# A scheduler that starts its TensorE clock at one half, and five first memsets moved from VectorE to GpSimd

## The chip, the cores and the metric

The kernel runs on one core of a Trainium2 chip. Its time is the device time of one execution in microseconds (us). It was taken several times for each kernel; "span" is the time from the first to the last instruction in a profiled execution and is about 1.8 us shorter. The granted clock is the share of TensorE's full clock that the throttle granted, as the profile records it.

TensorE, written PE in the profile, multiplies matrices. VectorE is DVE, ScalarE is ACT, GpSimd is POOL, and SyncE (SP) issues transfers. PEld is TensorE's loading of weights.

## The reference

Two layers, each attention and then a gated feed-forward block, on 2048 rows of 512 numbers, 32 heads of 16:

```python
def _A_ref(x, wqkv, wo):                       # 32 heads, Dh = 16
    q, k, v = split(x @ wqkv)
    p = softmax(einsum("bhqd,bhkd->bhqk", q, k) * Dh ** -0.5)
    return merge(einsum("bhqk,bhkd->bhqd", p, v)) @ wo
def _B_ref(x, w_gate, w_up, w_down):           # F = 1792
    return (gelu(x @ w_gate) * (x @ w_up)) @ w_down
for _ in range(2):
    x = x + _A_ref(layernorm(x), A_wqkv, A_wo)
    x = x + _B_ref(layernorm(x), B_w_gate, B_w_up, B_w_down)
```

(`split` and `merge` stand for the reshapes and transposes, which are cut.)

## The kernel before

The kernel isn't written as a fixed order of instructions. A greedy list scheduler, in Python, models all engines and decides at each modelled moment what TensorE does next; the order that comes out is fixed when the program is built. A wrong cost in the model therefore makes no wrong result. It makes a different order.

Two parts matter here. The first is the model of TensorE's clock: in windows of 3.413 us it counts the work done, and the next window runs at full rate only if the last one was busy for at least 42.5%.

```python
HAM, LEAST, BACK = 3.413, 0.425, 0.425
ham = {"n": 0, "act": 0.0, "rate": 1.0}        # the first window's rate
...
def ham_to(n):
    while ham["n"] < n:
        share = ham["act"] / HAM
        ham["rate"] = 1.0 if share >= (LEAST if ham["rate"] == 1.0 else BACK) else 0.5
        ham["n"] += 1
        ham["act"] = 0.0
def pe_time(t, work):
    while True:
        ham_to(int((t + 1e-6) // HAM))
        end = (ham["n"] + 1) * HAM
        can = (end - t) * ham["rate"]
        if work <= can:
            ham["act"] += work
            return t + work / ham["rate"]
        ham["act"] += can
        work -= can
        t = end
```

The second is what TensorE does when nothing is ready. It multiplies zeros into the accumulator bank, to keep its clock up. One call makes a group of four matmuls, side by side on four column strips of the array, 512 columns each:

```python
def keep_clock():
    ones = AP(ONB, 0, [[128, 128], [0, 4], [1, 128]])
    def fn(e):
        for j in range(4):
            ins = e.matmul(PS[32 * j:32 * j + VW, ACC, :], lhsT=ZV[:, :], rhs=ones, start=False, stop=False,
                           tile_position=(0, 32 * j), skip_group_check=True)
        return ins
    pe(fn, [("ZV",), ("ONB",)], [BK[ACC]], MM, "col")      # MM = 0.216 us at full rate
...
# in the main loop, when no tile, no product and no piece of work is ready:
if acc["free"] and not over[0] and density(t) < DENSE and ...:     # DENSE = 0.7
    keep_clock()
```

The head of the kernel is a chain. Four row tiles of x (128 rows each) are loaded; VectorE takes their statistics; GpSimd makes the layernorm scales, two tiles at a time; VectorE applies them; TensorE transposes the rows; then come the first projections to K, Q and V, and the first products of Q and K. Only then can ScalarE start its first exp. The initial memsets stood on VectorE in front of those statistics:

```python
sch.op("dve", lambda e: e.memset(PS[:, ACC, :], 0.0), w=[BK[ACC]], cost=0.6)
sch.op("dve", lambda e: e.memset(AP(VP, 16, [[NKT * H * VW, 128], [VW, NKT * H]]), 1.0), w=[("VPONE",)], cost=0.6)
sch.op("dve", lambda e: e.memset(RB[:], 0.0), ...)
sch.op("dve", lambda e: e.memset(OKL[:], 1.0), ...)
sch.op("dve", lambda e: e.memset(OKV[:], 1.0), ...)
sch.op("dve", lambda e: e.memset(LT[:], 1.0), ...)
```

## Time and profile before

| | before |
|---|---|
| time, median | 1685.6 us (1682.91 to 1685.63, 3 runs) |
| span of the profiled run | 1682.9 us |
| ScalarE busy | 1561.6 us, 93% |
| first exp starts | 17.67 us |
| last exp ends | 1610.1 us |
| after it (output projection, last feed-forward) | 72.7 us |

The first view is the page. Its first part gives busy time, share of the span and instruction count per engine. The groups of its fifth part give line, engine, operation, output and inputs, shapes, count, busy time, mean ns of one, and idle time before them.

```profile
span 1682.9 us, 37093 instructions
...
PE 1576.2 (94%) x15611; PEld 492.6 (29%) x15670; DVE 1378.6 (82%) x2334; ACT 1561.6 (93%) x1348; POOL 203.4 (12%) x217
...
L1204 ACT ACTIVATE fPT<-fPS 128x1536 bf16<-128x1536 f32 (+1 forms) x1302 | 1487.9, 1284 | 46.3 <-PE fPS L1191 42.5
...
```

ScalarE does the exps for nearly the whole span (L1204), and TensorE feeds it. So what delays the first exp delays everything, unless some slack later takes it up.

The second view is the chain of waits of the kernel before over its first 20 us (start, length, what): the work that ended last, followed backwards.

```profile
1.52 10.41 PE fPS L1344 x141
11.93 0.55 PE fPS L569 x8
...
17.67 2.37 ACT fPT L1204 x2
```

Of the 17.67 us before the first exp, 10.41 are the dummy matmuls of L1344. The timeline of the same stretch (start, length, engine, line, operation, tiles, count, and in brackets the idle time before it and what ended that) shows what they covered:

```profile
1.52 10.41 PE L1344 MATMUL fPS<-fONB,fZV 128*17 128x512 f16 x144 [1.52 <-POOL fQMASK L362]
...
3.86 0.91 DVE L369 MEMSET fRB<- 128x1024 f32 x1
...
4.99 0.63 DVE L540 BATCH_NORM_STATS2 fST<-fX 128x6 f32<-128x512 bf16 x1
...
5.76 0.15 PEld L1344 LDWEIGHTS fPS<-fONB,fZV 128*17 128x17 f16 x4 [0.28 <-issue]
...
6.18 0.15 PEld L1344 LDWEIGHTS fPS<-fONB,fZV 128*17 128x17 f16 x4 [0.28 <-issue]
...
6.59 4.85 PEld L1344 LDWEIGHTS fPS<-fONB,fZV 128*17 128x17 f16 x92 [0.25 <-issue]
...
8.14 0.72 DVE L562 TENSOR_SCALAR fHT<-fX,fLNS 128x512 f16<-128x512 bf16 x2
...
9.78 0.74 DVE L562 TENSOR_SCALAR fHT<-fX,fLNS 128x512 f16<-128x512 bf16 x2 [0.92 <-POOL fLNS L552]
...
11.87 0.62 PE L569 MATMUL fPS<-fIDN,fHT 128*128 128x128 f16 x8
...
```

The reader should see three things. The weight loads of dummy groups come every 0.43 us (5.76, 6.18) until 6.6 us, after which 92 of them pass in 4.85 us, that is a group of four every 0.21 us: TensorE ran at half rate at first. The first two tiles' rows were normalised between 8.14 and 8.86 us. The transposes (L569) that need them started at 11.87, as the dummies ended.

### The profile page before, as it was taken

To read this page: it belongs to the slowest core of one execution; us is meant where nothing else is said; L and a number is where in the kernel's file an instruction comes from. 1 tells how busy PE (TensorE), PEld (TensorE's weight loads), DVE (VectorE), ACT (ScalarE), POOL (GpSimd) and SP (SyncE) were. 2 spreads that over 40 slices of the span, in tenths; PEclk is the share of its full clock that TensorE was granted. 3 is DMA by queue.
4 is the path that set the end of the run, shared out by engine and by line. 5 is a ranking of instruction groups with operands and counts; after the bars stand their busy time and mean duration, and the time that the engine had idled before them with its cause. 6 is when DMAs were issued, how large, how long until landed. Compare 5 with 4: busy or idle time off the path is not lost.

```text
span 1682.9 us, 37093 instructions
## 1 busy us (share of the span) xinstructions
PE 1576.2 (94%) x15611; PEld 492.6 (29%) x15670; DVE 1378.6 (82%) x2334; ACT 1561.6 (93%) x1348; POOL 203.4 (12%) x217
## 2 busy tenths in 40 slices
PE   9999989999999989999999999999989999999998
PEld 3332222222222223233332322222222222222233
DVE  7899998888998899977643899988899878897852
ACT  6899999999999999999899999999999999999922
POOL 2312011101201021000600211101011100201000
PEclk9999999999999999999999999999999999999999
DMA  4100001252013410125214000024301251014303
GB/s 138 52 2 19 2 19 33 61 164 73 17 43 119 144 42 10 41 66 170 74 57 138 26 19 17 21 58 136 108 19 39 68 166 57 17 45 146 109 15 109
DMA packets 140286, 111.82 MB, mean 66 GB/s; under 512 B 13905, under 2 KB 129873, under 8 KB 140113
## 3 DMA queue, kind: packets, MB, share of 16 engines
q1 hardware_dynamic: 136416, 104.78, 21.3%
q0 software_dynamic: 2112, 4.19, 0.9%
q8 instruction: 127, 2.08, 0.5%
q10 hardware_dynamic: 1584, 0.39, 0.1%
q14 instruction: 47, 0.38, 0.1%
HBM read 97.78 MB, written 6.82 MB: 62 GB/s over the span
## 4 chain that ended last, share of the span: by engine, by line
ACT 52%; PE 35%; DVE 10%; DMA 1%; issue 1%; SPq 1%; POOL 0%; POOLq 0%; DVEq 0%
ACT fPT L1204 49%; PE fPS L592 11%; PE fPS L1324 9%; PE fPS L1191 9%; DVE fPP L1277 4%; PE fPS L953 4%; DVE fPI L1241 3%; ACT fHT L1157 2%; PE fPS L1344 2%; DVE fHT L939 1%; SPq L277 1%; DVE fHT L916 1%; ACT L1157 1%; PE fPS L656 1%; DVE fQ L636 0%
## 5 line engine op out<-in xcount | busy, mean ns | idle before, releaser
L1204 ACT ACTIVATE fPT<-fPS 128x1536 bf16<-128x1536 f32 (+1 forms) x1302 | 1487.9, 1284 | 46.3 <-PE fPS L1191 42.5
L1241 DVE TENSOR_SCALAR fPI<-fPS 128x512 int16<-128x512 f32 x843 | 571.0, 684 | 93.4 <-PE fPS L1191 87.6
L1191 PE MATMUL fPS<-fQ,fKT 32*128 32x512 f16 x4096 | 513.2, 384 | 50.0 <-ACT fPT L1204 36.3
L1324 PE MATMUL fPS<-fPT,fVP 128*17 128x512 bf16 x3253 | 469.0, 382 | 11.7 <-DVE fOS L829 5.6
L1277 DVE TENSOR_SCALAR fPP<-fPI 128x2048 int16<-128x2048 int16 (+3 forms) x723 | 444.7, 645 | 8.1 <-PE fPS L1324 2.3
L1324 PE MATMUL fPS<-fPP,fVD 128*17 128x512 f16 x2529 | 409.7, 381 | 10.8 <-DVE fPP L1277 5.9
L1191 PEld LDWEIGHTS fPS<-fQ,fKT 32*128 32x128 f16 x4096 | 129.0, 91 | 533.7 <-ACT fPT L1204 382.4
L1324 PE MATMUL fPS<-fPI,fVP 128*17 128x512 f16 x843 | 255.0, 382 | 2.0 <-DVE fPP L1277 1.5
L592 PE MATMUL fPS<-fXNT,fWR 128*128 128x512 f16 x896 | 221.7, 381 | 10.4 <-DVE fHT L939 6.0
L1344 PE MATMUL fPS<-fONB,fZV 128*17 128x512 f16 x2452 | 189.6, 385 | 2.3 <-POOL fQMASK L362 1.5
L1324 PEld LDWEIGHTS fPS<-fPT,fVP 128*17 128x17 f16 x3253 | 108.7, 88 | 163.4 <-issue 91.6
L788 POOL TENSOR_TENSOR fAT<-fOS,fRB 128x512 f16<-128x512 f32 x32 | 41.3, 1291 | 817.2 <-DMA fRB<-rscr 791.6
L1324 PEld LDWEIGHTS fPS<-fPP,fVD 128*17 128x17 f16 x2529 | 99.3, 88 | 120.7 <-issue 48.5
L939 DVE TENSOR_TENSOR fHT<-fPS,fHT 128x512 bf16<-128x512 f32 x112 | 76.4, 689 | 57.8 <-PE fPS L592 41.4
L953 PE MATMUL fPS<-fWR,fHT 128*128 128x512 bf16 x402 | 113.5, 382 | 7.2 <-issue 5.7
L592 PEld LDWEIGHTS fPS<-fXNT,fWR 128*128 128x128 bf16 x896 | 72.8, 98 | 128.3 <-DVE fHT L939 19.6
L916 DVE CAST fHT<-fPS 128x512 bf16<-128x512 f32 x98 | 66.6, 687 | 25.6 <-PE fPS L592 25.2
L1344 PEld LDWEIGHTS fPS<-fONB,fZV 128*17 128x17 f16 x2452 | 57.8, 91 | 66.5 <-issue 31.2
L1324 PEld LDWEIGHTS fPS<-fPI,fVP 128*17 128x17 f16 x843 | 58.3, 88 | 38.0 <-issue 13.9
L669 POOL TENSOR_SCALAR fVD<-fVP 128x544 f16<-128x544 f16 (+1 forms) x48 | 54.7, 1142 | 97.0 <-DVE fVP L677 94.4
L548 POOL TENSOR_SCALAR fLNS<-fMV 128x4 f32<-128x4 f32 (+1 forms) x17 | 5.2, 307 | 434.8 <-DVE fMV L541 434.7
L788 POOL TENSOR_TENSOR fATS<-fOS,fRB 128x512 f16<-128x512 f32 x32 | 42.3, 1323 | 78.2 <-DMA fRB<-rscr 78.2
(60 smaller groups left out, 697.9 us busy)
## 6 DMA issues: line engine op xcount, KB each, us to landing
fWR<-in_B_w_down_dram SPq DMA_DIRECT2D x189, 256.0 KB, 3.0
fWR<-in_B_w_gate_dram SPq DMA_DIRECT2D x56, 256.0 KB, 3.3
fWR<-in_B_w_up_dram SPq DMA_DIRECT2D x56, 256.0 KB, 2.9
fRB<-rscr SPq DMA_DIRECT2D x256, 32.0 KB, 1.8
fX<-in_A_x_dram POOLq DMA_DIRECT2D x4, 1024.0 KB, 5.6
xscr<-fX SPq DMA_DIRECT2D x16, 256.0 KB, 2.5
fX<-xscr SPq DMA_DIRECT2D x4, 1024.0 KB, 5.7
fAT<-fATS SPq DMA_DIRECT2D x128, 16.0 KB, 1.8
```

Of the source, the lines that this page charges most:

```text
L592: ins = e.matmul(bank(bs[0])[:, 0:cols], lhsT=l, rhs=r_, start=(i == 0), stop=(i == n - 1))
L669: job("pool", 2, [(lambda e, dst=dst, src=src, ph=ph: e.tensor_scalar(dst, src, 2.0 ** (-ph / NPH), None, op0=ALU.mult), [("VP", c, k) for ...
L788: job("pool", 1, [(lambda e: e.tensor_tensor(dst, OS[:, os_, :], RB[:, slot, :], op=ALU.mult), [("OS", os_)] + [("RB", slot, j) for j in r ...
L916: evac_job(1, b, [(lambda e: e.tensor_copy(HT[:, ft, :], bank(b)), [BK[b]], [("HT", ft)], 0.6)], got(("gate", layer, qb, ft)))
L939: (lambda e: e.tensor_tensor(HT[:, ft, :], bank(b), HT[:, ft, :], op=ALU.mult), [BK[b], ("HT", ft)], [("HT", ft)], 0.62)], got(("up", laye ...
L953: ins = e.matmul(bank(b)[:, 0:D], lhsT=HT[:, ft, i * 128:(i + 1) * 128], rhs=WR[:, s, jj * D:(jj + 1) * D], start=(ft == 0), stop=(ft == N ...
L1191: ins = e.matmul(bank(b), lhsT=KT[32 * j:32 * j + 32, (u % NG) // 2, kt * 128:(kt + 1) * 128], rhs=Q[32 * j:32 * j + 32, (layer * NU + u) ...
L1204: o = sch.op("act", lambda e: e.activation(PT[:, p, 0:512 * na].rearrange("p (a b) -> p a b", a=na), PS[:, b0:b0 + na, :], ACTF.Exp, scale ...
L1241: dve(0, [(lambda e: e.tensor_scalar(PI[:, gi, 512 * r:512 * (r + 1)], bank(bd), DBIAS, 0.0, op0=ALU.add, op1=ALU.max), [BK[bd]], [("PI", ...
L1277: shifts.append((s, [(lambda e: e.tensor_scalar(PP[:, s, 0:512 * n], PI[:, gi, 0:512 * n], int(OCT) * ph // NPH, None, op0=ALU.add), [("PI ...
L1324: ins = e.matmul(PS[32 * j:32 * j + VW, ACC, :], lhsT=l, rhs=r_, start=a, stop=z, tile_position=(0, 32 * j), skip_group_check=True)
L1344: ins = e.matmul(PS[32 * j:32 * j + VW, ACC, :], lhsT=ZV[:, :], rhs=ones, start=False, stop=False, tile_position=(0, 32 * j), skip_group_c ...
```

## The change

Its intent is to make the model's clock true to the chip over the first microseconds, and to let VectorE reach its first statistics sooner. It is six lines:

```diff
-    ham = {"n": 0, "act": 0.0, "rate": 1.0}
+    ham = {"n": 0, "act": 0.0, "rate": 0.5}
...
     sch.op("dve", lambda e: e.memset(PS[:, ACC, :], 0.0), w=[BK[ACC]], cost=0.6)
-    sch.op("dve", lambda e: e.memset(AP(VP, 16, [[NKT * H * VW, 128], [VW, NKT * H]]), 1.0), w=[("VPONE",)], cost=0.6)
-    sch.op("dve", lambda e: e.memset(RB[:], 0.0), w=[("RB", i, j) for i in range(NRB) for j in range(4)], cost=0.6)
-    sch.op("dve", lambda e: e.memset(OKL[:], 1.0), w=[("OKL",)])
-    sch.op("dve", lambda e: e.memset(OKV[:], 1.0), w=[("OKV",)])
-    sch.op("dve", lambda e: e.memset(LT[:], 1.0), w=[("LT", i) for i in range(HB)])
+    sch.op("pool", lambda e: e.memset(OKV[:], 1.0), w=[("OKV",)])
+    sch.op("pool", lambda e: e.memset(AP(VP, 16, [[NKT * H * VW, 128], [VW, NKT * H]]), 1.0), w=[("VPONE",)], cost=0.9)
+    sch.op("pool", lambda e: e.memset(OKL[:], 1.0), w=[("OKL",)], cost=0.2)
+    sch.op("pool", lambda e: e.memset(LT[:], 1.0), w=[("LT", i) for i in range(HB)], cost=0.2)
+    sch.op("pool", lambda e: e.memset(RB[:], 0.0), w=[("RB", i, j) for i in range(NRB) for j in range(4)], cost=0.9)
```

## The prediction

> **What bounds the kernel now.** ScalarE, fed by TensorE. On the page ScalarE is busy 1561.6 of 1682.9 us (93%), 1487.9 of it in 1302 exps; the chain that ended last is 49% exps and about 35% TensorE. From 17.7 to 1627 us (windows) ScalarE idles about 60 us. Outside lie the head (the first exp starts at 17.67 in the timeline) and a tail of 56 us that TensorE bounds.
>
> **What the change is.** A greedy list scheduler that models every engine emits the kernel. One initial value of its model changes, and five memsets change engine. No arithmetic changes, but the order of instructions may change everywhere.
>
> **The memsets.** In the timeline the five cost VectorE 485+912+165+62+165 ns = 1.8 us, from 3.24 to 5.08 us; the first statistics follow at 4.99. GpSimd is idle from 2.38 to 6.72. From its own memsets (91 ns for one element per partition, 120 for 17, 200 for 128) I estimate about 2.0 us for the five, done by 4.5 us, before its first layernorm scaling. But the statistics need x, whose first transfers take a median of 3.4 us from issues that begin at 0.80, so I expect them only about 0.8 us earlier.
>
> **The clock.** The granted clock reads 1.00 from the start, yet the dummy matmul groups (four matmuls of 512 columns, side by side) start every 0.43 us until 6.6 us and every 0.21 after. The Trainium skill ("TensorE: Matmul & The Clock Gate", What's actually happening) says that half rate is the default and activity releases it; the trace agrees. The model believed full rate from zero and put 144 dummy matmuls before the first transposes: TensorE runs them from 1.52 to 11.93, while the first normalised rows were ready at 8.86. With half rate each group counts double, so about 18 groups (60 to 90 matmuls) go in front: 12 at 0.43 and 6 at 0.21 us end near 8 us. Transposes then start with the rows, at 8.1 to 8.9; the second rows come at about 9.8 instead of 10.5, the projections at 11 to 12 instead of 14.5, the first exp at about 14.5, three microseconds earlier. From 17.67 to 47.5 ScalarE runs nearly without a gap, so this is on the critical path.
>
> Against it: the model may stay at half rate for several windows, order the first exps badly and let vector tiles in later: 0.5 to 1 us back. And the remaining order is reshuffled: the tile split (3253 matmuls from ScalarE, 843 from VectorE directly) may shift, one tile being worth 0.43 us of ScalarE, and so may its idle time. This scatter is larger than the head's gain.
>
> **Prediction.** 1685.6 - 3 = about 1682.5 us; eight times in ten 1672 to 1692. Faster by over 2%: 1%; within 2%: 98%; slower by over 2%: 1%.
>
> **What would show it.** 60 to 90 dummy matmuls before the first transposes, transposes at 8 to 9 us, first exp at 14 to 15.5; the memsets on GpSimd 1.7 to 2.5 us together; first statistics at about 4.2. If these hold and the time differs, the difference lies in the reshuffled body: counts of tiles, ScalarE's idle time.
>
> **What would make it wrong.** TensorE going cold again after 8 us for want of dummies (projections at 0.43 us a matmul); x or weights landing too late (DMA is full from 3.4 to 17.7 us); or a reshuffle worth over 10 us.

## The result, and the profile after

The changed kernel took 1682.79 us (median of 4 runs, 1678.73 to 1686.26). Before took 1685.37 us beside it (4 runs, 1682.91 to 1685.63). All outputs are right. Ratios and intervals in this document compare the means of both kernels' runs, so they aren't quite the ratio of the medians quoted. Here the ratio is 0.9984 with a 95% interval of 0.9965 to 1.0004: the same time, within what four runs can tell.

The page after, lines answering to those of before:

```profile
span 1680.1 us, 36981 instructions
...
PE 1574.3 (94%) x15555; PEld 490.9 (29%) x15614; DVE 1378.3 (82%) x2329; ACT 1561.3 (93%) x1348; POOL 208.6 (12%) x222
...
L1204 ACT ACTIVATE fPT<-fPS 128x1536 bf16<-128x1536 f32 (+1 forms) x1302 | 1487.6, 1286 | 49.1 <-PE fPS L1191 45.5
...
```

ScalarE's work is the same, to 0.3 us. The program lists say more: compared instruction by instruction, the two kernels differ in two places only. TensorE has 88 dummy matmuls ahead of its first transposes instead of 144, and five memsets stand in GpSimd's list instead of VectorE's. **Every other instruction of every engine stands in the same order.**

The chain of waits after, over the first 20 us:

```profile
...
2.18 4.51 DMA fX<-in_A_x_dram
...
6.72 0.70 DVE fST L540
...
8.08 0.75 POOL fLNS L550
...
9.64 0.72 PE fPS L569 x8
...
14.70 5.97 ACT fPT L1204 x5
```

The long run of dummies has left the chain. It now begins with the landing of the fourth row tile of x at 6.69 us, and leads over its statistics and scales to the second transposes at 9.64. The timeline after:

```profile
1.52 6.78 PE L1344 MATMUL fPS<-fONB,fZV 128*17 128x512 f16 x88 [1.52 <-POOL fQMASK L362]
...
2.45 2.31 POOL L369 MEMSET fVP<- 128x512 f16 x1
...
3.35 0.70 DVE L540 BATCH_NORM_STATS2 fST<-fX 128x6 f32<-128x512 bf16 x1 [1.88 <-DMA fX<-in_A_x_dram]
...
4.93 0.98 POOL L372 MEMSET fRB<- 128x1024 f32 x1
...
5.97 0.24 POOL L548 TENSOR_SCALAR fLNS<-fMV 128x2 f32<-128x2 f32 x1
...
6.72 0.69 DVE L540 BATCH_NORM_STATS2 fST<-fX 128x6 f32<-128x512 bf16 x1 [0.62 <-DMA fX<-in_A_x_dram]
...
8.23 0.62 PE L569 MATMUL fPS<-fIDN,fHT 128*128 128x128 f16 x8
...
```

The first exp starts at 14.70 instead of 17.67 us, so the head is 2.97 us shorter; the span is 2.8 us shorter. That looks like a perfect match. The experiments show that the match is partly luck.

### The profile page after: what moved, and what is told of

Same layout as the page of the kernel before. It is cut to its first block, busy times and chain, and to the rows that moved or that the text cites. A ratio compares the mean times of both kernels' runs of the same rounds, so it can differ in the third digit from the quotient of the medians.

```text
span 1680.1 us, 36981 instructions
## 1 busy us (share of the span) xinstructions
PE 1574.3 (94%) x15555; PEld 490.9 (29%) x15614; DVE 1378.3 (82%) x2329; ACT 1561.3 (93%) x1348; POOL 208.6 (12%) x222
## 4 chain that ended last, share of the span: by engine, by line
ACT 53%; PE 34%; DVE 10%; POOL 1%; DMA 1%; issue 1%; SPq 0%; DVEq 0%; POOLq 0%
ACT fPT L1204 50%; PE fPS L592 10%; PE fPS L1324 9%; PE fPS L1191 8%; DVE fPP L1277 4%; PE fPS L953 3%; DVE fPI L1241 3%; PE fPS L1344 2%; ACT fHT L1157 2%; POOL fVD L669 1%; DVE fHT L916 1%; DVE fHT L939 1%; ACT L1157 1%; PE fPS L656 1%; DVE fQ L636 0%
## 5 line engine op out<-in xcount | busy, mean ns | idle before, releaser
L1204 ACT ACTIVATE fPT<-fPS 128x1536 bf16<-128x1536 f32 (+1 forms) x1302 | 1487.6, 1286 | 49.1 <-PE fPS L1191 45.5
L1277 DVE TENSOR_SCALAR fPP<-fPI 128x2048 int16<-128x2048 int16 (+3 forms) x723 | 445.5, 646 | 8.1 <-PE fPS L1324 2.4
L788 POOL TENSOR_TENSOR fAT<-fOS,fRB 128x512 f16<-128x512 f32 x32 | 43.1, 1345 | 815.6 <-DMA fRB<-rscr 815.6
L592 PEld LDWEIGHTS fPS<-fXNT,fWR 128*128 128x128 bf16 x896 | 72.8, 98 | 128.9 <-DVE fHT L939 19.6
L788 POOL TENSOR_TENSOR fATS<-fOS,fRB 128x512 f16<-128x512 f32 x32 | 42.4, 1325 | 78.2 <-DMA fRB<-rscr 78.2
```

Of the source, the lines that this page charges most:

```text
L592: ins = e.matmul(bank(bs[0])[:, 0:cols], lhsT=l, rhs=r_, start=(i == 0), stop=(i == n - 1))
L788: job("pool", 1, [(lambda e: e.tensor_tensor(dst, OS[:, os_, :], RB[:, slot, :], op=ALU.mult), [("OS", os_)] + [("RB", slot, j) for j in r ...
L1204: o = sch.op("act", lambda e: e.activation(PT[:, p, 0:512 * na].rearrange("p (a b) -> p a b", a=na), PS[:, b0:b0 + na, :], ACTF.Exp, scale ...
L1277: shifts.append((s, [(lambda e: e.tensor_scalar(PP[:, s, 0:512 * n], PI[:, gi, 0:512 * n], int(OCT) * ph // NPH, None, op0=ALU.add), [("PI ...
```

## The experiments

**Theory A:** surplus dummy matmuls held the first transposes back; the clock setting takes them out; that is the gain, and it is carried to the end. **Theory B:** the memsets on VectorE held the head back. **Theory C:** the head doesn't count, and the 2.6 us are scatter.

One table holds the head, the body and the tail of all profiled runs. The head ends as the first exp starts, the body as the last exp ends; all three are worked out from the timelines' starts and ends. The column "full rate" is when the spacing of weight loads falls from 0.43 us, to about 0.3 us or less, read from the timeline (a dash: no run of full dummy groups to read it from).

| run | dummies ahead of the transposes | full rate at | head | body | tail | span |
|---|---|---|---|---|---|---|
| before | 144 | 6.6 | 17.67 | 1592.5 | 72.7 | 1682.9 |
| before_again | 144 | 7.0 | 17.88 | 1595.3 | 71.6 | 1684.8 |
| memsets_only | 144 | 4.1 | 16.46 | 1596.5 | 72.0 | 1684.9 |
| clock_only | 88 | 7.0 | 15.30 | 1593.6 | 70.6 | 1679.5 |
| after | 88 | 5.3 | 14.70 | 1594.9 | 70.5 | 1680.1 |
| after_again | 88 | 7.0 | 15.45 | 1593.6 | 71.2 | 1680.2 |
| memset_order | 88 | 7.5 | 15.09 | 1594.3 | 72.2 | 1681.6 |
| no_dummies | 22 short ones | - | 15.90 | 1596.0 | 71.0 | 1683.0 |
| half_dummies | 44 and 11 short ones | 4.8 | 17.28 | 1595.2 | 72.8 | 1685.3 |
| more_dummies | 488 | 7.4 | 36.56 | 1591.3 | 70.6 | 1698.5 |
| early_x | 88 | 6.6 | 14.65 | 1591.1 | 70.8 | 1676.6 |
| late_and_early | 88 | 6.2 | 18.83 | 1594.5 | 70.8 | 1684.1 |
| late_early_trim | 68 and 5 short ones | 6.1 | 18.50 | 1592.0 | 70.9 | 1681.4 |
| busy_gpsimd | 88 | 6.6 | 15.00 | 1628.3 | 71.0 | 1714.4 |

### The two halves of the change, and both kernels again

`clock_only` changes the one rate and leaves the memsets on VectorE; `memsets_only` moves the memsets and leaves the rate.

```diff
 # clock_only, on the kernel before
-    ham = {"n": 0, "act": 0.0, "rate": 1.0}
+    ham = {"n": 0, "act": 0.0, "rate": 0.5}
 # memsets_only, on the changed kernel
-    ham = {"n": 0, "act": 0.0, "rate": 0.5}
+    ham = {"n": 0, "act": 0.0, "rate": 1.0}
 # before_again, after_again: no edit
```

> The model's first rate alone, memsets left on VectorE. Theory A (the surplus dummy matmuls held the transposes back, so the clock setting is the larger part): 88 dummies end near 8.3 us, first transposes at 8.6 to 8.9, second ones at about 10.25 behind the second rows, first exp at 15.3 us, 2.4 us earlier than before's 17.67. Theory B (the memsets on VectorE held the head back): first exp stays near 17.5. Theory C (nothing in the head counts; the difference is scatter): the first exp moves as A says but the span doesn't follow at all. The whole time should lie 2.4 us under before by A, with a scatter of 2 to 3 us per run.

> The memsets moved to GpSimd alone, rate 1.0 as before: 144 dummies. Theory A: the dummies still end at 11.93 us, so the first exp stays at 17.67 (within 0.1 us) although the statistics start at 3.3 us; time as before. Theory B: first exp at about 15 us, time 2.5 us less.

> The changed kernel as it is, timed again over five rounds: first exp at 14.7 us, 0.15% (2.6 us) under before. The five spans should scatter by some us, less where the mean granted clock is 1.000 than where it is 0.997; its order of instructions is the same each time, so any difference between two of its traces in the body is scatter.

> The kernel before, for a second trace. Head within 0.1 us of the first trace's (first exp 17.67). If the differences of up to 2 us that open and close in the body between before and after come from chance and not from the change, two traces of before itself, which have the same order, show the same: steps of 0.3 to 1 us at places where a VectorE instruction of 685 ns takes 1 us or more while GpSimd works. If the change caused them, these two traces keep within 0.3 us of each other.

Measured: clock_only 1681.64 us (4 runs, ratio to before 0.9994, 0.9973 to 1.0014); memsets_only 1686.32 us (4 runs, 1.0009, 0.9992 to 1.0027); after_again 1683.28 us (6 runs, 0.9994, 0.9979 to 1.0010); before beside them 1685.09 us (11 runs, 1680.60 to 1687.41). All are the same within 2%. None is told from before.

The timelines of clock_only and then of memsets_only, the dummies and the first exps:

```profile
1.52 7.68 PE L1344 MATMUL fPS<-fONB,fZV 128*17 128x512 f16 x88 [1.52 <-POOL fQMASK L362]
...
15.30 24.96 ACT L1204 ACTIVATE fPT<-fPS 128x1536 bf16<-128x1536 f32 x22 [4.03 <-PE fPS L1191]
...
```

```profile
1.52 9.20 PE L1344 MATMUL fPS<-fONB,fZV 128*17 128x512 f16 x144 [1.52 <-POOL fQMASK L362]
...
16.46 24.05 ACT L1204 ACTIVATE fPT<-fPS 128x1536 bf16<-128x1536 f32 x21 [3.90 <-PE fPS L1191]
...
```

Setting the clock alone brings the first exp to 15.30 us, as theory A put it to the hundredth, though not all of the way there was as it said: the dummies ended at 9.20 us and not near 8.3, while the second transposes, which led on, came at 10.23 (10.25 expected). The memsets alone bring 16.46, which neither theory had: A had said 17.67. The reason lies in the lines. The same 144 dummies took 9.20 us here and 10.41 in before, and the 1.21 us between them are all of the 1.21 us that the first exp gained. Full rate came at 4.1 us here and at 6.6 in before; at 0.43 against 0.21 us a group, the six groups passed at full rate instead of half make 1.3 us. So moving the memsets brought nothing of its own here; the chip's clock was released earlier in this execution.

That release is a matter of chance: with the same first instruction at 1.52 us, the 13 traces of the table that show it have it between 4.1 and 7.5 us. The Trainium skill ("TensorE: Matmul & The Clock Gate", What's actually happening) says the activity window of 3.4 us is free-running and doesn't start with the kernel, which fits a spread of 3.4 us. It also gives the variation of the transition as ±500 ns; here it is over three times as wide. (A later remark in the same section, that one kernel showed 6, 11 or 14 slow matmuls depending on the phase, is nearer to what is seen here.)

So before's head swings with the clock's phase, since 144 dummies stand in front of everything. After's swings less: 88 dummies end between 8.3 and 9.4 us, close to the time at which the rows are ready. In after_again the first exp came at 15.45, as full rate came late (7.0) and the fourth tile of x landed later, its statistics starting at 7.46 instead of 6.72. The heads of clock_only (15.30) and of three profiles of both parts (14.70, 15.45 and, in a variant below, 15.09; mean 15.08) don't differ beyond that swing. Theory B falls; the memsets' share is at most some tenths and stays unresolved.

The repeats also answer the question of the body. Two profiles of the very same program differ by 2.9 us in the body (before 1592.5, before_again 1595.3). If the n-th exp's start in one trace is set against the n-th in another, the difference drifts as it goes:

| start of the exp in before, us | 17.7 | 134.5 | 490.5 | 728.8 | 1090.8 | 1336.4 | 1572.7 | 1609.4 |
|---|---|---|---|---|---|---|---|---|
| after, difference | -2.97 | -2.98 | -2.68 | -1.51 | -0.67 | -1.96 | -2.51 | -0.60 |
| after_again, difference | -2.22 | -2.22 | -1.55 | -0.41 | +1.01 | -0.37 | -1.19 | -1.15 |
| before_again, difference | +0.20 | +0.20 | +0.63 | +0.50 | +0.85 | +1.73 | +2.07 | +3.05 |

After's lead was down to 0.67 us at two thirds and to 0.60 at the last exp. The 2.2 us that were missing came back in the tail, which was 70.5 us long against 72.7. Tails of all runs lie between 70.5 and 72.8 whatever the kernel, so the near match of 2.97 and 2.8 us in the first pair is a coincidence of the body's and the tail's scatter.

### What the dummies ahead of the transposes are worth

All three kernels change only what the first 22 calls of `keep_clock` emit. The model isn't told, so all orders stay.

```diff
 def keep_clock():
+    k = dummies[0]; dummies[0] += 1
+    short = LO <= k < HI          # no_dummies 0, 22; half_dummies 11, 22; more_dummies none
+    more = MORE if k == 21 else 0 # more_dummies 100, else 0
     def fn(e):
-        for j in range(4):
+        if short:
+            return e.matmul(PS[0:VW, ACC, 0:8], lhsT=ZV[:, :], rhs=ONB[:, 0:8], ...)
+        for i in range(4 * (1 + more)):
+            j = i % 4
             ins = e.matmul(...)
```

> The changed kernel with its first 22 dummy groups cut to one matmul of 8 columns each, all else in the same order. Theory A in its strong form (dummies are only a cost once the rows could be there): transposes at 8.2 us as in after, first exp at 14.7 or earlier. Rival (the dummies before the first transposes buy the full rate for the chain behind them): the array is at half rate at 8.2 us, the matmuls of K and Q start every 0.43 us instead of 0.21, V's and the transposes take twice as long, until a busy window has passed; I estimate 2 to 3 us from these counts, so first exp at 17 to 18 us and the time near before's.

> The changed kernel with dummy groups 12 to 22 cut to 8 columns: 11 full groups, over by about 6.2 us, then TensorE idles about 2 us until the rows are there. If the rate once released holds over such a gap: first exp at 14.7 to 15.3 and the dummies of 6.2 to 8.3 us are of no use. If it falls back (or was never released): half rate at the transposes and projections, first exp at 16.5 to 18.

> The changed kernel with 100 more dummy groups (400 matmuls) ahead of the first transposes. At 0.216 us a group this is 21.6 us, far above the scatter. If the body follows the head one to one (as the equal order says): first exp at 36.0 to 36.8 us, time 21.6 us over after's, that is near 1704. If the body takes up a late start (DMA further ahead, slack in ScalarE's 60 us of idle time): less than 20 us.

Measured: no_dummies 1684.28 us (4 runs, ratio 1.0003, 0.9986 to 1.0019), half_dummies 1682.48 us (4 runs, 0.9991, 0.9974 to 1.0007), more_dummies 1700.80 us (4 runs, 1.0106, 1.0089 to 1.0123), before beside them 1683.92 us (7 runs). The timelines of no_dummies and of half_dummies:

```profile
8.56 1.04 PE L569 MATMUL fPS<-fIDN,fHT 128*128 128x128 f16 x8 [6.34 <-DVE fHT L562]
...
12.71 1.04 PE L592 MATMUL fPS<-fXNT,fWK 128*128 128x512 f16 x4
...
15.90 24.96 ACT L1204 ACTIVATE fPT<-fPS 128x1536 bf16<-128x1536 f32 x22 [4.44 <-PE fPS L1191]
...
```

```profile
1.52 4.09 PE L1355 MATMUL fPS<-fONB,fZV 128*17 128x512 f16 x44 [1.52 <-POOL fQMASK L362]
...
8.45 1.04 PE L569 MATMUL fPS<-fIDN,fHT 128*128 128x128 f16 x8 [2.59 <-DVE fHT L562]
...
13.32 1.81 PE L592 MATMUL fPS<-fXNT,fWK 128*128 128x512 f16 x4
...
17.28 24.05 ACT L1204 ACTIVATE fPT<-fPS 128x1536 bf16<-128x1536 f32 x21 [5.93 <-PE fPS L1191]
...
```

Eight transposes take 1.04 us here and 0.62 in after: TensorE is at half rate. Without dummies the first exp comes at 15.90 us, 0.4 to 1.2 us later than with 88 of them (14.70 to 15.45); I had said 17 to 18, because I expected half rate to last through the projections, and it ended at about 12 us (the K projections of 12.71 take 1.04 us, as in after). With half of the dummies it is worse, 17.28: full rate came at 4.8 us, the dummies ended at 5.9, and TensorE then idled 2.6 us and was back at half rate at 8.45, until nearly 15 us (K took 1.81 us). The skill's table at the same place puts the fall back to half rate at one idle window of about 3.4 us or more. The length of the idle stretch alone doesn't decide it here: TensorE was at half rate after 2.6 us of idleness in half_dummies, but in late_early_trim, a variant below, it still ran at full rate directly after 3.31 us of it (each of the transposes at 11.84 took 0.22 us, against 0.31 at half rate in half_dummies) and only later fell back:

```profile
11.84 0.71 PE L569 MATMUL fPS<-fIDN,fHT 128*128 128x128 f16 x8 [3.31 <-DVE fHT L562]
...
14.47 1.88 PE L592 MATMUL fPS<-fXNT,fWK 128*128 128x512 f16 x4
...
```

What fits is a decision at the ends of windows of 3.4 us that run on regardless of the work. In half_dummies, late_and_early and late_early_trim the matmuls' records put the first release at about 4.7, 6.2 and 6.0 us and the return to full rate at about 14.9, 16.4 and 16.2, each time 10.2 us later, which is three such windows; in the last two, half rate began at about 12.9, two windows after the release. So an idle window needn't be wholly idle: half_dummies ran its dummies for about 1.2 us of the 3.4 after the release. This is worked out from the three traces; no run was made to test it.

So the strong form of theory A falls. Dummies have a use in the head as long as they reach up to the moment the rows are ready; beyond it they're a cost. That rests on one trace each of no_dummies and half_dummies, with the clock's phase as it fell; the total time resolves neither of these two heads.

more_dummies asks whether the head is carried to the end, with a delay far above the scatter:

```profile
36.56 3.71 ACT L1204 ACTIVATE fPT<-fPS 128x1536 bf16<-128x1536 f32 x3 [3.90 <-PE fPS L1191]
...
```

Its first exp came at 36.56 us, 18.9 us later than in before's first profile and 21.1 to 21.9 later than in the two of after. The difference of the mean times to before is 1.06%, 17.8 us. That is 94% of 18.9, and the 1.1 us that are missing are within the body's scatter of 2 to 3 us. I had said 1704 us and it was 1700.8. Against the changed kernel, from which it differs by the 400 dummies alone, the account is weaker: a delay of 21.1 to 21.9 us in the first exp stands against 17.5 to 18.0 us between the medians, or 18.8 to 20.5 by the two ratios to before. My expectation had put less than 20 us as the mark of a body that takes up part of the delay, so that isn't excluded; the two kernels weren't run side by side. Theory C falls: most of a head delay, some 80 to 97% of it, reaches the end. That all of it does isn't shown.

### The order of GpSimd's memsets

```diff
-    OKV, VP (every 17th element), OKL, LT, RB
+    OKV, RB, OKL, LT, VP (every 17th element)
```

> The changed kernel with the two large GpSimd memsets in swapped order (zeros of 128x1024 second, ones of the value columns last). In after the value columns' memset took 2.31 us, my estimate was 0.53. If the shape (every 17th element of two bytes) costs it: again about 2.3 us in its new place, and 1.0 us for the other. If the place costs it (first large one, or while VectorE works): the zeros now take over 2 us and the value columns about 0.5.

The timeline of memset_order:

```profile
2.45 0.96 POOL L369 MEMSET fRB<- 128x1024 f32 x1
...
3.63 2.30 POOL L372 MEMSET fVP<- 128x512 f16 x1
...
```

The strided memset takes 2.30 us last and 2.31 first, the plain one 0.96 and 0.98. The shape costs it, not the place. VectorE did the same strided memset in 0.48 us.

### A shorter head: an attempt, and what it ran into

After the change the chain says that the fourth row tile of x comes too late. `early_x` issues the third and fourth tiles first on ScalarE's queue. `late_and_early` also moves the four larger memsets behind the first scales, since in after the memsets ended at 5.91 us and the first scale began at 5.97 although its statistics were ready at 5.18. `late_early_trim` cuts the last 5 of the 22 groups besides.

```diff
 # early_x
-        dma("sp", "ldx0_%d" % t, xb(t), ...)
+        dma("sp" if t < 2 else "act", "ldx0_%d" % t, xb(t), ...)
 # late_and_early: as early_x, and
+    def late_memsets():           # VP, OKL, LT and RB on GpSimd, as in the change
...
         if b + 1 < NQB:
-            head_stats(b + 1)
+            head_stats(b + 1); b or late_memsets()
 # late_early_trim: as late_and_early, with LO, HI = 17, 22 in keep_clock
```

> The changed kernel with the third and fourth row tiles of x issued first on ScalarE's queue instead of third and fourth on SyncE's. Theory (after the change the head is bound by the landing of the fourth row tile at 6.7 to 7.5 us, as the chain of waits says): its issue comes at 1.3 instead of 2.2 us, the fourth statistics start about 1 us earlier, second transposes at 8.8 to 9.3 instead of 9.6 to 10.4 unless the dummies, which end between 8.3 and 9.2, hold the first ones; first exp at 14.0 to 14.8. If DMA bandwidth and not the order of issue bounds it: no earlier than 14.7.

> early_x plus the four larger memsets on GpSimd moved behind the first block's layernorm scaling, so that the first scaling needn't wait for them (in after it began at 5.97, as the memsets ended at 5.91, while its statistics were ready at 5.2). First scaling at 5.2, first rows at 6.8; then the 22 dummy groups, over at 8.3 to 9.2 by the phase of the warm-up, bind again: first exp at 14.0 to 15.1, 0.3 us or so better than early_x. Time 0 to 1 us under after.

> late_and_early with 17 instead of 22 full dummy groups (the last 5 cut to 8 columns), over at 7.2 to 8.1 us. First transposes there, second ones at 8.6 to 8.9, first exp at 13.6 to 14.0: a head 0.8 to 1.5 us shorter than after's, 3.7 to 4.1 shorter than before's. In the whole time that is 0.2% under before, at the edge of what five rounds tell apart; if the array falls back to half rate in the shorter cover, first exp near 16.

Measured: early_x 1678.32 us (one look, state unknown); late_and_early 1685.00 us (4 runs, ratio 0.9995, 0.9980 to 1.0009); late_early_trim 1683.14 us (6 runs, 0.9986, 0.9973 to 0.9999); before beside them 1684.45 us (11 runs, 1683.31 to 1687.21).

The timeline of early_x:

```profile
1.52 7.39 PE L1344 MATMUL fPS<-fONB,fZV 128*17 128x512 f16 x88 [1.52 <-POOL fQMASK L362]
...
5.89 0.66 DVE L540 BATCH_NORM_STATS2 fST<-fX 128x6 f32<-128x512 bf16 x1
...
9.72 0.62 PE L569 MATMUL fPS<-fIDN,fHT 128*128 128x128 f16 x8
...
14.65 26.31 ACT L1204 ACTIVATE fPT<-fPS 128x1536 bf16<-128x1536 f32 x23 [3.89 <-PE fPS L1191]
...
```

The fourth statistics start at 5.89 instead of 6.72 to 7.46 us. The second transposes, though, come at 9.72: the 88 dummies took 7.39 us in this execution and hold the transposes again, as full rate came late. The first exp is at 14.65. That is in the range expected, at its upper half, and no better than after's best.

The other two failed, in a way worth seeing. This is late_and_early:

```profile
8.74 2.27 POOL L370 MEMSET fVP<- 128x512 f16 x1
...
8.84 3.59 DVE L562 TENSOR_SCALAR fHT<-fX,fLNS 128x512 f16<-128x512 bf16 x2 [0.93 <-POOL fLNS L552]
...
```

The two layernorm applications of L562 took 3.59 us; in after two of them took 0.73. They run beside GpSimd's late memsets. The Trainium skill ("SBUF — State Buffer", Who interferes with whom) says VectorE and GpSimd share a pair of ports to SBUF as an exclusive lock, and that `tensor_scalar` can enter a mode that needs it; whoever issues first holds it and the other blocks. This agrees with it: the single VectorE instructions took 2.56 and 1.11 us instead of 0.4. The wait then let TensorE idle, the projection to K was at half rate again (1.74 us), and the first exp came at 18.83 us, 4 us later than expected. late_early_trim met the same at 8.34 us and has its first exp at 18.50. My reasoning was that nothing waits for these memsets so early. It looked at dependencies alone, and that was not enough. The interval of late_early_trim, 0.9973 to 0.9999, leaves out 1 by a hair although its profiled head is longer than before's: with effects this small such an interval alone proves little.

### Where the body's scatter comes from

In after, the lead over before shrinks by 0.9 us at 1044 us. The timelines of after and then of before at the same place:

```profile
...
1041.69 1.27 POOL L788 TENSOR_TENSOR fAT<-fOS,fRB 128x512 f16<-128x512 f32 x1 [1.76 <-DMA fRB<-rscr]
...
1041.92 3.13 DVE L1277 TENSOR_SCALAR fPP<-fPI 128x2048 int16<-128x2048 int16 x4
...
1044.55 1.45 ACT L1204 ACTIVATE fPT<-fPS 128x1536 bf16<-128x1536 f32 x1 [0.80 <-PE fPS L1191]
...
```

```profile
...
1042.35 1.27 POOL L788 TENSOR_TENSOR fAT<-fOS,fRB 128x512 f16<-128x512 f32 x1 [1.47 <-DMA fRB<-rscr]
...
1043.21 2.50 DVE L1277 TENSOR_SCALAR fPP<-fPI 128x2048 int16<-128x2048 int16 x4
...
```

In after the same four shifts (L1277) start 0.23 us behind a GpSimd product (L788) and take 3.13 us; the first of them alone took 1.60 us instead of 0.685, and it ended 0.55 us after the product did. ScalarE then idles 0.80 us. In before the product started 0.86 us ahead of them and was nearly over: the first shift took 0.95 us, and the four 2.50. GpSimd's product is released by a small transfer that lands (the bracket in a trace says so: `fRB<-rscr`), so its start wanders against VectorE's from run to run.

Over whole traces (counted from the records of VectorE and GpSimd): before has 34 VectorE instructions more than 0.15 us over the median of their shape, 18.8 us over it together; after has 33 with 20.0 us. **All of them run beside a GpSimd instruction**, and those beside L788 make 16.5 and 17.8 us of it. The order of the starts decides who waits: in the 24 shifts of 128x2048 that were long beside L788 in before, and the 23 in after, the product had begun first every time, and the shift ended 0.55 us after it. Shifts that began first kept their 0.68 to 0.70 us, and the product took 1.28 to 1.77 us instead of 1.27. To test this, `busy_gpsimd` does each of the 64 products of L788 twice, with the same result:

```diff
-  job("pool", 1, [(lambda e: e.tensor_tensor(dst, OS[...], RB[...], op=ALU.mult), [...], wk, 1.35)], done)
+  job("pool", 1, [(lambda e: e.tensor_tensor(dst, OS[...], RB[...], op=ALU.mult), [...], wk, us)
+                  for us in (0.0, 1.2)], done)      # the model's time for both stays 1.35
```

> The changed kernel with each of GpSimd's 64 normalising products of 128x512 done twice (same values), so GpSimd has 82 us more work; the orders of all other engines stay. Theory on the scatter of the body (VectorE's shifts of 128x2048, 0.685 us alone, wait for GpSimd products that run at the same time): their time over the median rises from 17 to 20 us to 28 to 40 us, all of it beside a GpSimd instruction, and the stretch from first to last exp grows by 2 to 6 us from 1592 to 1595. Rival (the long ones have another cause and the overlap is chance): the excess stays at 17 to 20 us.

Measured: 1711.96 us (4 runs, ratio 1.0158, 1.0143 to 1.0173). The groups of L1277 of 128x2048, with their busy time and mean, first in after and then in busy_gpsimd:

```profile
L1277 DVE TENSOR_SCALAR fPP<-fPI 128x2048 int16<-128x2048 int16 x555 | 381.5, 716 | 4.8
...
```

```profile
L1277 DVE TENSOR_SCALAR fPP<-fPI 128x2048 int16<-128x2048 int16 x555 | 402.9, 755 | 4.8
...
```

The shifts' mean rises from 716 to 755 ns, all long VectorE instructions together from 33 with 20.0 us to 65 with 46.6 us over the median, again every one beside GpSimd. That is more than the 28 to 40 us I had expected. The body grows by 33.5 us (1594.9 to 1628.3), far over the 2 to 6 us expected. I had taken most of VectorE's waiting to vanish in slack; instead ScalarE's idle time before its exps grew by 30 us (page and groups: 49.1 to 79.1). This kernel also delays each product's readers by 1.27 us, and its granted clock is lower (0.993 to 0.995), so not all of the 33.5 us is shown to be the collision. What is shown is that the long VectorE instructions come with GpSimd's products and grow with them. The other 13 traces point the same way: their bodies, 1591.1 to 1596.5 us long, are the longer the more time over the median such instructions cost within them (17.8 to 22.3 us), with a correlation of 0.85 and about 1 us of body for each us. A correlation is not an experiment, but it covers most of the spread.

No kernel without such collisions was run, so how much of the body's scatter (2.9 us between the two traces of before, 5.4 us over the 13) would remain without them stays open. Whether the clock has a part in it too is not shown: the four runs of the changed kernel have spans of 1676.9, 1680.1, 1681.8 and 1684.5 us at mean granted clocks of 1.000, 0.998, 0.999 and 0.997. With the whole page of before at 0.999, its windows show 1.00 in every stretch to 1627 us and 0.97 in the tail. Other kernels' runs don't follow this neatly (after_again has 1679.1 and 1683.0 us, both at 1.000).

## Why the prediction was right or wrong

The number was right: 1682.5 predicted, 1682.79 measured. The range held, and the forecast "within 2%" held. But that 0.3 us is luck. Single runs of the same program spread by up to 7.5 us, and the 10 runs of the changed kernel taken in two sets give ratios of 0.9984 and 0.9994, that is 1.0 to 2.7 us, neither clear of zero. What stands is the head: 14.70 to 15.45 us in four profiles with 88 dummies and otherwise the order of the change (after, after_again, clock_only, memset_order), against 16.46 to 17.88 in three with 144.

- **What bounds the kernel:** right. ScalarE's 1561 us didn't change, and more_dummies showed that a later first exp is a later end.
- **The surplus dummies:** right in kind. 144 became 88, within the 60 to 90 predicted; transposes at 8.23 us in after (8 to 9 predicted; 9.13 in after_again, as full rate came late), projections at 11.48 (11 to 12), first exp at 14.70 and 15.45 (14 to 15.5).
- **"About 18 groups" and "the model may stay at half rate for several windows":** the count was 22. Printing the model's own times shows that it stays at half rate for two windows only, to 6.83 us, emits 14 groups until then and 8 at full rate, and stops.
- **"The remaining order is reshuffled" and "this scatter is larger than the head's gain":** wrong as to its cause. This is the step that failed. The order of everything behind the first transposes is identical. In both versions the model finds no rows ready until 9.5 us of its own time, has stopped its dummies by 8.6, and goes on from the same state. The scheduler forgot the difference, because all its engines then waited for the same event. The scatter exists and is as large as the gain, but it lies in the execution of one fixed order: in the collisions of VectorE with GpSimd for most of it, as far as the traces tell, and perhaps in the clock.
- **The memsets:** the estimate of 2.0 us was too small. They ran from 2.41 to 5.91 us. The strided one took 2.31 us instead of about 0.5, and so they were not "done by 4.5 us, before its first layernorm scaling": they held that one back by about 0.8 us. The statistics began at 3.35, 1.6 us earlier and not 0.8, but then waited 0.62 us for the fourth tile. Neither had much effect on the first exp.
- **"TensorE going cold again for want of dummies":** it didn't happen in after. It did in half_dummies, late_and_early and late_early_trim, with half rate in the projections as described.

early_x took 1678.32 us, less than every run of before (1680.60 at best). It is a single look, its head is no shorter than after's best, its body (1591.1) is short within the scatter, and single runs of the changed kernel (1678.73) and of late_early_trim (1678.16) came as low. I don't call it faster. No version was found that beats before clear of the scatter.

## What to carry to other kernels

If a scheduler places filler work by a model, check the filler against the trace at the first place where real work waits behind it: here one wrong initial value put 10.4 us of dummies in front of rows that were ready at 8.9. Before you fear or hope for a reshuffle from a changed model, compare the instruction lists; they may be equal from the first common wait on. And before moving work to an idle GpSimd, look at what VectorE does in the same microseconds and not only at who needs the result, because the two can block each other.

## What the Trainium skill lacked or had wrong

- "TensorE: Matmul & The Clock Gate", What's actually happening: the transition is said to vary by ±500 ns. With the first matmul always at 1.52 us, full rate came between 4.1 and 7.5 us in 13 traces. The section's own count of 6, 11 or 14 slow matmuls for one kernel already says more than ±500 ns.
- The same section's table: back to half rate after one idle window of about 3.4 us or more. It lacks how idle a window has to be. half_dummies was back at half rate after 2.6 us of idle TensorE (5.86 to 8.45 us), late_early_trim still at full rate after 3.31 us (8.53 to 11.84).
- "TensorE: Matmul & The Clock Gate" warns that throttle events in traces are unreliable (Seeing it yourself), but doesn't say that a granted clock can read 1.00 while the array runs at half rate: in before's first windows it reads 1.00 with dummy groups every 0.43 us.
- "GPSIMD Engine Reference", Performance pitfalls for Q7 kernels, gives the extra cost of strided reads (+50%). A memset that writes every 17th two-byte element took 2.30 us for 512 elements per partition, a plain one of 1024 elements 0.96 us; VectorE took 0.48 us for the strided one.
- "SBUF — State Buffer", Who interferes with whom, agrees with the traces. It gives no size for a whole kernel: here 31 to 37 VectorE instructions a run were long beside it, by 17.8 to 25.1 us in all, and 65 by 46.6 us when GpSimd's products were doubled.
- No page explains why VectorE's second instruction, which waits for no semaphore, began at 3.23 to 3.25 us in before, before_again and clock_only, 1.77 to 1.78 us after its first had ended. The runs don't either.
